# Three second products of a gated feed-forward kernel: from f32 passes to split f16 passes, with low parts added by transfers, and a new program order

## The chip, the cores and the metric

The kernel runs on one core of one Trainium2 chip. A core has TensorE (PE, matrix products; its weight loads are listed as PEld), VectorE (DVE), ScalarE (ACT), GpSimd (POOL) and SyncE (SP, which issues most transfers), each with its own in-order instruction queue; they meet through semaphores. The metric is the device time of one execution in microseconds (us), as a median of several runs. One further execution was taken with the profiler; all rows below come from it.

## What is computed

```python
# q, k, v, f_logit: (4 batches, 8 heads, 768 steps, 48); w_in: (384, 2048); w_out: (2048, 384)
f = 1 / (1 + exp(-f_logit))
for t in range(768):
    state = f[:, :, t, :, None] * state + einsum('bhd,bhe->bhde', k[:, :, t], v[:, :, t])
    y[:, :, t] = einsum('bhd,bhde->bhe', q[:, :, t], state)
x = y.transpose(0, 2, 1, 3).reshape(3072, 384)
h = x @ w_in
out = (h * clip(h + 3, 0, 6) / 6) @ w_out
```

A gated linear attention makes the 3072 rows of `x`; a feed-forward layer with a hard-swish gate follows. Both are wanted in close to f32 precision.

## The kernel before

**Tiling.** The 768 steps are cut into 6 chunks of 128, which with 4 batches gives 24 attention units (0 to 23). Four units, one chunk of all batches, make one group of 512 rows for the feed-forward layer, so there are groups 0 to 5. The 2048 hidden columns are cut into 16 tiles of 128.

**Split precision.** TensorE takes f16 operands in one pass. A f32 operand is therefore held as two f16 parts, `high` (the rounded value) and `low` (the value less its high part), and a product is the sum of three f16 passes: high by high, low weight by high, high weight by low (`P3`). `mm1` (L664) makes a hidden tile so, with 9 matmuls over three blocks of 128 inputs; `relu` (ACT, L674) and `g` (DVE, L678) apply the gate into a f32 tile `t`; `gh` (ACT, L683) makes the high part of `t`, `gl` (DVE or POOL, L693) the low part; `mm2` (L709) multiplies by the 384 outputs, again 9 matmuls of 128x512. Each group's outputs sum up in three PSUM banks `o`, tile after tile.

**The first group.** While attention starts, weights still have to be converted: `ld` loads a weight tile, `z`, `cy`, `mid`, `dif` and `top` turn it into f32 in `wide`, `high` (ACT, L317) and `low` (L320) make its f16 parts; `lowi` and `lowo` make the low part of the first or the second product's columns alone. In group 0, tiles 0 to 4 run in two halves of 256 rows with a second product in f32 (L846), tiles 5 to 7 run whole with a second product in f32 as well: `mm2x` (`mm2_whole`, L720), 3 f32 matmuls of 128x512 straight from `wide` and `t`, each of which stands in the trace as 2 records. Such a tile needs neither `gh` and `gl` nor a low part of its output weights. From tile 8 on, `mm2` takes over. Groups 2 to 5 take another form of the first product (L772, 128x256).

**Attention.** A unit is `tk` (transposes, L516), `kv` (L537), `att` (L497), `qs` (L571) and `av` (L587) on PE, with 16 to 32 small f32 matmuls each, and `mask`, `carry`, `decay` on other engines. `att`, `kv` and `qs`/`av` share two pairs of PSUM banks. While a `qs` has begun to accumulate into a pair, `hold` puts a no-op on PE that waits for PE's own earlier matmul before another step writes that pair.

**The order.** The whole program is one hand-written list of tokens, `ORDER`: it sets the order on every engine, and the number at a token's end says which PSUM bank it takes. `ON_POOL` names the steps that run on POOL. At the end `seed.1` multiplies a block of zeros into a bank (L809), `count` (L985) sums the self-tests of the program, `judge` (L988, L991) decides on a slow fallback, which does not run here. `outs`/`outv`/`outh` copy results out of PSUM, `od`/`odh` send them to memory.

Of the kernel before, what the change touches and what calls it, by code (L numbers as in the profile page):

```python
# [69 lines left out]
mm1.5.4 mask.5 mm2b.4 carry0.6 xh.4 z.7 xl.4 mid.6 dif.6 kmul.7 carry1.6 loadv.5 kv.5.3 ld.8 relu.5 g.5 mm2x.5 cy.7  # L70
top.6 high.6 cy.8 rend.7 tk.7.0 mid.7 dif.7 load.8 lowi.6 carry0.5 top.7 mm1.6.4 ktok.7 qs.5.2 fwd.7 qmul.7 high.7
loadv.7 relu.6 g.6 z.8 decay.7 att.6.0 ld.9 lowi.7 gate.8 av.5 cy.9 z.9 mask.6 mm1.7.4 relu.7 mid.8 dif.8 top.8 mid.9
carry1.5 dif.9 high.8 low.8 mm2x.6 mm1.8.0 g.7 loadq.8 ld.10 top.9 xh.5 cy.10 relu.8 high.9 back.8 rend.8 mm2x.7 ld.11
xl.5 g.8 att.7.2 z.10 cy.11 qs.6.0 kv.7.3 mid.10 load.10 loadv.8 av.6 dif.10 low.9 top.10 z.11 mid.11 gh.8 mm1.9.4
# [5 lines left out]
hole.6 hole.5 mm1.16.4 load.9 mid.15 mm1.17.1 relu.16 carry1.8 relu.17 dif.15 ws1.0 g.16 mm1.20.0 g.17 loadq.11 low.14  # L80
gate.10 xtop.0 gate.9 mm1.18.1 load.11 top.15 relu.18 loadq.10 back.9 high.15 gh.16 av.8 back.10 mm1.14.4 g.18 mm2.13
lowo.4 gh.17 relu.14 low.15 g.14 gh.14 mm1.15.1 mm1.19.4 lowo.6 gh.18 kmul.9 gl.18 rend.9 relu.15 g.15 lowo.3 gh.15
gl.14 gl.15 tk.9.1 lowo.5 lowo.1 mm2.14 fwd.9 mm2.15 gl.16 ktok.9 gl.17 outs.2 loadv.11 lowo.7 outv.1 outs.0 mm1.23.1
mm2.16 gate.11 lowo.2 ws2.0 relu.19 od.0 ws3.0 mm2.17 rend.10 xh.8 g.19 back.11 od.2 kmul.10 relu.20 decay.9 relu.23
kmul.11 hole.8 fwd.10 rend.11 od.1 load.13 qmul.10 xsum.0.2 g.20 g.23 mm1.21.4 relu.21 load.12 xleast.0 tk.10.3 ws4.0
qmul.9 decay.10 ktok.10 mm2.18 gh.19 g.21 mm1.25.3 gh.20 mm1.24.2 gh.21 loadv.10 gate.12 wtop.4 gl.19 relu.24 att.9.1
relu.25 kv.9.0 gl.20 fwd.11 g.25 carry0.9 loadv.12 g.24 wsh.0 load.14 qmul.11 mm1.22.4 gate.13 relu.22 back.12 gh.24
mm2.19 tk.11.3 gl.21 ws1.1 mask.9 gh.23 carry1.9 ktok.11 mm2.20 g.22 qs.9.0 att.11.3 gate.14 loadq.12 gh.25 gl.25 av.9
att.10.2 mm2.21 back.13 gh.22 xh.9 gl.23 kv.11.0 rend.12 kv.10.1 gl.22 mask.10 loadq.13 decay.11 mm1.26.4 ws2.1
mask.11 carry0.10 qs.10.3 ws3.1 carry0.11 carry1.10 kmul.12 kmul.13 fwd.12 qs.11.1 av.10 av.11 relu.26 mm2.22 ws4.1  # L90
xh.10 xh.11 decay.12 rend.13 mm1.27.3 gl.24 carry1.11 relu.27 loadq.14 decay.13 fwd.13 tk.12.2 mm1.28.1 relu.28 hole.9
ktok.12 wsl.0 ws1.2 g.27 tk.13.0 mm2.23 qmul.12 qmul.13 wsh.1 hole.10 att.13.3 ws2.2 g.26 ktok.13 g.28 xtop.1 att.12.1
t0.4 loadv.13 kv.12.2 kv.13.0 back.14 carry0.13 load.15 hole.11 load.16 xsum.1.4 carry0.12 gh.26 mm2.24 gh.27 mm2.25
t0.5 mask.13 carry1.12 t1.4 t1.5 seed.0.2 kmul.14 mm1.30.3 gh.28 t2.4 ws3.2 xleast.1 carry1.13 t2.5 th.4 ws4.2 gate.15
mask.12 gl.26 gl.27 wsl.1 th.5 ws1.3 mm2.26 tl.4 mm1.29.1 tk.14.2 relu.30 mm1.31.0 tl.5 relu.29 rend.14 g.30 p1.8.4
loadv.14 ktok.14 ws2.3 relu.31 p7.8.2 g.29 wsh.2 cs.8 ca.8.2 loadv.17 mm2.27 g.31 p6.8 gh.29 gate.16 fwd.14 qs.13.0
xtop.2 cx.8.3 qs.12.1 p2.8 wsl.2 ws3.3 ra.8 back.15 gl.28 p5.8 av.13 av.12 mm2.28 gh.31 gaw.8 loadq.15 loadq.17 gh.30
ws4.3 rend.15 load.17 ce.8 wsh.3 p4.8 qmul.14 gl.30 gl.29 xh.13 xh.12 p3.8 p8.8 rb.8 rx.8 p7.9.1 decay.14 wsl.3 mm2.29
gl.31 kmul.15 loadq.16 re.8 tk.15.0 gew.8 cs.9 p1.9.4 gbw.8 ca.9.2 mm2.30 fwd.15 loadv.15 gxw.8 back.16 ktok.15
xsum.2.1 mm2.31 p6.9 qmul.15 p7.11.0 xmost.2 gh.33 gh.34 cs.11 xleast.2 p2.9 decay.15 gl.34 hole.13 gh.32 kv.15.1  # L100
kv.14.0 kmul.16 cx.9.3 gl.32 outs.5 load.18 ra.9 hole.12 carry0.14 carry1.14 p4.9 carry0.15 outs.3 carry1.15 p5.9 rx.9
att.14.0 gaw.9 att.15.1 ce.9 outv.4 gate.17 p8.9 mask.14 rend.16 p3.9 mask.15 gh.35 gate.18 qs.15.0 back.17 re.9
qs.14.1 gxw.9 fwd.16 kmul.17 gl.33 gl.35 mm2.32 av.14 av.15 gew.9 p7.10.3 xh.15 rend.17 loadq.18 mm2.33 mm2.34 t0.6
p1.10.4 rb.9 mm2.35 gbw.9 qmul.16 fwd.17 xh.14 loadv.16 back.18 gh.37 gh.38 rend.18 cs.10 decay.16 load.19 kmul.18
ca.10.2 gl.38 hole.15 p6.10 gh.36 tk.17.0 gl.37 p2.10 hole.14 decay.17 tk.16.1 gh.39 cx.10.3 gl.36 p4.10 t1.6 gate.19
fwd.18 ra.10 gaw.10 t2.6 ktok.17 p5.10 ktok.16 att.16.0 kv.16.1 mm2.36 ce.10 t0.7 qmul.17 p8.10 load.20 rx.10 re.10
load.21 qmul.18 back.19 loadv.18 p3.10 mm2.37 rb.10 mask.16 gew.10 carry0.16 carry1.16 p1.11.4 gbw.10 gh.40 att.17.0
gxw.10 kv.17.1 t1.7 th.6 loadq.19 ca.11.2 gl.40 gl.39 mm2.38 gh.42 p6.11 t2.7 carry0.17 xtop.3 carry1.17 gl.42 gate.21
wtop.3 th.7 p2.11 rend.19 tl.6 mm2.39 cx.11.3 gate.20 mm2.40 mask.17 ra.11 gaw.11 tl.7 p4.11 gh.43 rx.11 p5.11 ce.11
tk.18.1 p7.13.0 p8.11 gh.41 gxw.11 gl.43 ktok.18 cs.13 gl.41 xsum.3.3 wtop.8 p3.11 qs.17.1 rb.11 qs.16.0 mm2.41  # L110
loadq.20 re.11 av.17 xmost.3 loadv.19 av.16 xleast.3 p7.12.3 gbw.11 gh.46 gew.11 xh.16 gh.45 p1.12.4 ca.12.2 xh.17
gl.45 mm2.42 loadv.23 att.18.1 kv.18.0 decay.18 gh.44 p2.12 p6.12 back.20 gl.46 cs.12 mm2.43 cx.12.3 carry0.18 gl.44
mask.18 p4.12 ra.12 p5.12 kmul.19 fwd.19 gaw.12 gh.47 mm2.44 decay.19 load.22 ce.12 loadv.22 od.5 back.21 carry1.18
gl.47 rx.12 qmul.19 p3.12 mm2.45 rb.12 p8.12 mm2.46 kmul.20 re.12 gxw.12 qs.18.0 gbw.12 gew.12 hole.16 gh.48 p1.13.4
# [1124 lines left out]
```

## Time and profile before

| | us |
|---|---|
| three runs, median | 456.95 |
| lowest and highest of them | 456.78, 457.9 |
| profiled execution, its own time | 457.2 |
| its span, from the first instruction to the last | 455.5 |
| PE busy | 448.7 (99%) |
| DVE busy | 358.3 (79%) |
| ACT busy | 231.2 (51%) |
| POOL busy | 18.7 (4%) |

Matmuls are pipelined: one lasts longer in the trace than the distance at which the next one starts. How much of PE's time a step takes is therefore read as the distance between its start and the start of the step behind it, not from its duration.

### The profile page before, as it was taken

The numbers are of one execution on the slowest core, as the hardware profiler recorded it, in microseconds if no ns is written. First come the engines' busy times: TensorE is split into PE (matmuls) and PEld (weight loads), VectorE is DVE, ScalarE is ACT, GpSimd is POOL, SyncE is SP. The second block draws the span as 40 slices with busy tenths as digits, with TensorE's granted clock in tenths as the row PEclk, the third lists the DMA queues.
The fourth block names the chain that finished last, engine by engine and source line by source line (L and its number), as shares of the span: only waits on it lengthen the run. The fifth ranks groups of instructions, "written<-read, shape, count | busy, mean of one in ns | idle before, by whom it ended". The sixth has DMA issues, their size and how long they took to land.

```text
span 455.5 us, 12559 instructions
## 1 busy us (share of the span) xinstructions
PE 448.7 (99%) x5449; PEld 291.5 (64%) x5449; DVE 358.3 (79%) x643; ACT 231.2 (51%) x389; POOL 18.7 (4%) x31
## 2 busy tenths in 40 slices
...
PEclk9999999999999999999999999999999999999999
...
GB/s 284 221 257 388 221 192 250 204 167 4 52 130 95 164 47 76 92 3 121 89 1 85 83 150 6 22 142 2 1 10 1 5 30 2 1 115 2 1 0 73
DMA packets 25531, 43.18 MB, mean 95 GB/s; under 512 B 2560, under 2 KB 17408, under 8 KB 25472
## 3 DMA queue, kind: packets, MB, share of 16 engines
...
q14 instruction: 16, 0.13, 0.1%
...
## 4 chain that ended last, share of the span: by engine, by line
PE 96%; DVE 2%; ACT 1%; issue 0%; DVEq 0%; ACTq 0%
PE o L709 35%; PE pair L772 16%; PE single L772 9%; PE pair L664 7%; PE single L664 5%; PE pair L497 3%; PE o L846 3%; PE pair L587 3%; PE pair L571 3%; PE pair L537 2%; PE idle L1071 2%; PE o L720 2%; PE pair L516 2%; PE pair L862 1%; PE o_half L862 1%; PE single L828 1%
## 5 line engine op out<-in xcount | busy, mean ns | idle before, releaser
L709 PE MATMUL o<-gg,weight 128*128 128x512 f16 x744 | 173.4, 379 | 0.0
L709 PEld LDWEIGHTS <-weight 128*128 128x128 f16 x744 | 71.7, 98 | 73.8
L772 PEld LDWEIGHTS <-weight 128*128 128x128 f16 x672 | 65.1, 98 | 13.3 <-issue 0.2
L772 PE MATMUL pair<-xmem,wide 128*128 128x256 f16 x384 | 51.2, 273 | 0.0
L683 ACT ACTIVATE gg<-raws 128x512 f16<-128x512 f32 x64 | 38.4, 624 | 23.9 <-DVE raws L806 8.1
L772 PE MATMUL single<-xmem,weight 128*128 128x256 f16 x384 | 49.8, 273 | 0.2 <-DVE raws L806 0.2
L801 ACT ACTIVATE raws<-pair,half 128x512 f32<-128x512 f32 x32 | 21.5, 684 | 42.3 <-PE pair L772 33.3
L772 PEld LDWEIGHTS <-wide 128*128 128x128 f16 x384 | 36.9, 98 | 8.7 <-DVE single L787 0.6
L801 ACT ACTIVATE raws<-single,half 128x512 f32<-128x512 f32 x32 | 22.0, 687 | 39.8 <-PE single L772 32.2
L664 PEld LDWEIGHTS <-weight 128*128 128x128 f16 x243 | 23.1, 98 | 26.7 <-issue 0.3
L772 PE MATMUL pair<-xmem,weight 128*128 128x256 f16 x288 | 36.5, 273 | 0.0
L806 DVE SCALAR_TENSOR_TENSOR raws<-raws,single 128x512 f32<-128x512 f32 x32 | 21.8, 682 | 18.3 <-ACT raws L801 18.3
L693 DVE TENSOR_TENSOR gg<-raws,gg 128x512 f16<-128x512 f32 x48 | 31.9, 683 | 5.0 <-ACT gg L683 5.0
L664 PE MATMUL pair<-xmem,weight 128*128 128x512 f16 x144 | 33.2, 379 | 0.0
L806 DVE SCALAR_TENSOR_TENSOR raws<-raws,pair 128x512 f32<-128x512 f32 x32 | 21.5, 682 | 12.3 <-ACT raws L801 12.1
L787 DVE TENSOR_TENSOR pair<-pair,raws 128x512 f32<-128x512 f32 x16 | 11.2, 697 | 25.3 <-PE pair L772 17.1
L448 DVE TENSOR_TENSOR_SCAN suffix<-gates,rend 112x516 f32<-112x516 f32 x24 | 29.6, 1235 | 0.1
L428 DVE TENSOR_TENSOR_SCAN suffix<-gates,unit 112x516 f32<-112x516 f32 x23 | 28.0, 1223 | 0.1
L664 PE MATMUL single<-xmem,weight 128*128 128x512 f16 x99 | 23.2, 380 | 0.0
L674 ACT ACTIVATE tg<-pair,half 128x512 f32<-128x512 f32 x16 | 10.9, 686 | 19.5 <-PE pair L664 16.3
L683 ACT ACTIVATE gg<-tg 128x512 f16<-128x512 f32 x24 | 14.4, 626 | 9.0 <-DVE tg L678 5.2
L504 DVE TENSOR_TENSOR a<-pair,causal 128x512 f32<-128x512 f32 x24 | 16.3, 684 | 2.3 <-PE pair L497 1.3
...
## 6 DMA issues: line engine op xcount, KB each, us to landing
...
raws<-w SPq DMA_DIRECT2D x16, 768.0 KB, 5.7
gates<-fg SPq DMA_DIRECT2D x23, 258.5 KB, 3.6
...
wide<-wide SPq DMA_DIRECT2D x32, 24.0 KB, 2.0
...
```

Source lines behind the costliest of these rows:

```text
L428: nc.vector.tensor_tensor_scan(flat(sf)[:, ::-1], gt[:, 1:][:, ::-1], flat(unit)[:, ::-1], 0.0, op0=ALU.mult, op1=ALU.add,)
L448: nc.vector.tensor_tensor_scan(flat(sf), gt[:, :NP * (C + 1)], flat(rend), 0.0, op0=ALU.mult, op1=ALU.add,)
L497: nc.tensor.matmul(d["at"][HC * odd:HC * (odd + 1), e, 2 * n + c], t[rs, 1, n, c, odd], t[rs, 0, n, c, odd], start=not growing[at], stop=T ...
L504: nc.vector.tensor_tensor(d["a"].rearrange("r p e t -> r e p t"), d["at"], causal.unsqueeze(1).unsqueeze(1).broadcast_to([128, 2, NP, HC]) ...
L571: nc.tensor.matmul(d["y"][to:to + 64, odd, n, cs], before[rs, p], t[rs, 0, n, c, odd], start=alone and (odd, e) not in seen, stop=False, s ...
L664: nc.tensor.matmul(h, win[:, f, a, k * 128:(k + 1) * 128], g["xt"][:, k, :g["n"] // C, b], start=i == 0, stop=i == 3 * KT - 1,)
L683: nc.scalar.activation(d["gg"][:, 0], d["t"], AF.Copy)
L693: engine("gl", int(g["name"]) * NF + f).tensor_tensor(d["gg"][:, 1], d["t"], d["gg"][:, 0], op=ALU.subtract)
L709: nc.tensor.matmul(g["o"][m], wout[:, f, a, m * 128:(m + 1) * 128], g[f]["gg"][:, b], start=f == 0 and i == 0, stop=f == NF - 1 and i == 2 ...
L772: nc.tensor.matmul(to[:, n * 256:(n + 1) * 256], weights(q, n, a), g["wide"][:, :, block - 3, b], start=fresh and count == 1, stop=count = ...
L801: nc.scalar.activation(to, src, AF.Relu, bias=half, scale=RISE)
L806: nc.vector.scalar_tensor_tensor(to, to, TOP, src, op0=ALU.min, op1=ALU.mult)
```

## The change

The tiles 5 to 7 of group 0 get the split second product `mm2` in the place of `mm2x`. What this needs is made by new means. `lno` (`conv_minus`) writes the negative of the output weights, rounded to f16, into the place of the low part, on ACT; `lowo` then adds the f32 weights to it by a transfer that POOL issues and that accumulates in its target. In the same way `gn` (`gneg`) writes the negative of `t`, rounded, on ACT, and `gl` adds `t` by such a transfer. There are six of these transfers (`ON_DMA`). `lowo.5` to `lowo.7` stood on DVE before, later in the program.

`apart` and `touch` are new: before a `qs` begins in a pair of banks, PE waits for its own last matmul of an `att`, `kv` or `av` in that pair. PE instructions that wait for PE number 22 before and 40 after.

The first 225 tokens of the order (up to `cy.6`) stay; all behind them stands in a new order. `seed.1` is gone. All else is the same set of steps, with the same banks. Lines behind L193 are up to 33 higher in the changed kernel: `mm2` is L742 there, `gh` L709, `relu` L700.

```diff
+ON_DMA = """
+gl.5 gl.6 gl.7 lowo.5 lowo.6 lowo.7
+""".split()
...
-top.5 cy.6 tk.6.1 ktok.6 mm2a.4 back.7 ld.7 decay.5 high.5 qs.4.2 decay.6 att.5.0 gb.4 av.4 kv.6.1 carry1.4 lowi.5
+top.5 cy.6 qs.4.2 carry1.4 gb.4 mid.6 ld.7 tk.6.1 ktok.6 high.5 cy.7 loadv.5 z.7 back.7 dif.6 decay.6 av.4 kv.5.3 top.6
...
+    def apart(at):
+
+        if touched[at] is not None:
+            after(nc.tensor.nop().ins, touched[at], mybir.DependencyClass.Sync)
+            touched[at] = None
+
+    def touch(at):
+        touched[at] = nc.cur_bb.bb.instructions[-1]
...
+    def conv_minus(f, half):
+        nc.scalar.activation(two(weight[:, f, 1])[:, half], both(f)[:, half], AF.Copy, scale=-1.0)
+
     def conv_low(op, f, half):
+        if f"{op}.{f}" in ON_DMA:
+            nc.gpsimd.dma_start(
+                out=two(weight[:, f, 1])[:, half], in_=both(f)[:, half], accum_op=ALU.add
+            )
+            return
...
         def qs():
             t = chunks[i]
             at, half = pair()
+            apart(at)
...
+    def gneg(g, f):
+        d = g[f]
+        nc.scalar.activation(d["gg"][:, 1], d["t"], AF.Copy, scale=-1.0)
+
     def glow(g, f):
         d = g[f]
+        if f"gl.{int(g['name']) * NF + f}" in ON_DMA:
+            nc.gpsimd.dma_start(out=d["gg"][:, 1], in_=d["t"], accum_op=ALU.add)
+            return
```

PE at the second product of tile 7 in group 0, before. `tg0_7` is the gated f32 tile, `o0_0` to `o0_2` are the group's output banks, L664 is a first product, L497 to L537 are attention.

```order
L664 LDWEIGHTS weight_75
L664 MATMUL pair0_70<-xmem_117,weight_75 128x512
L720 MATMUL o0_0_572<-tg0_7_1042,wide_73 128x512
L720 MATMUL o0_1_573<-tg0_7_1042,wide_73 128x512
L720 MATMUL o0_2_574<-tg0_7_1042,wide_73 128x512
L497 MATMUL pair1_71<-qkf7_792 64x64 x16
L571 MATMUL pair0_70<-qkf6_729,decayed0_104 64x64 x8
L571 MATMUL pair0_70<-qkf6_729,middle0_102 64x64 x8
L537 MATMUL pair1_71<-v7_985,ktok7_964 48x48 x16
```

PE in the changed kernel from the last matmul of tile 5 to the first of tile 8 (`gg0_5`, `gg0_8` are the split tiles; 9 matmuls of tile 8 and then 9 of tile 6, `gg0_6`, follow).

```order
L742 MATMUL o0_2_577<-gg0_5_975,weight_75 128x512
L519 MATMUL pair1_71<-qkf7_795 64x64 x16
L560 MATMUL pair1_71<-v7_931,ktok7_949 48x48 x16
L596 MATMUL pair0_70<-qkf6_732,decayed0_104 64x64 x8
L596 MATMUL pair0_70<-qkf6_732,middle0_102 64x64 x8
L742 LDWEIGHTS weight_75
L742 MATMUL o0_0_575<-gg0_8_1097,weight_75 128x512
```

Three f32 matmuls a tile have become nine f16 ones, and tile 6's stand behind tile 8's; only the last three of a tile's nine read the part that `gl` adds.

ACT in the changed kernel, where tile 6 gets its two parts: `tg0_8` is written by `relu.8`, which waits for the first product of tile 8; then come `gh.6` and `gn.6`, behind which the transfer `gl.6` is released.

```order
L332 ACTIVATE weight_75<-wide_73 128x384
L700 ACTIVATE tg0_7_1072<-single_72,half_95 128x512
L300 ACTIVATE wide_73<-raws_74 128x2x384
L700 ACTIVATE tg0_8_1077<-pair0_70,half_95 128x512
L709 ACTIVATE gg0_6_1089<-tg0_6_979 128x512
L713 ACTIVATE gg0_6_1089<-tg0_6_979 128x512
L709 ACTIVATE gg0_7_1092<-tg0_7_1072 128x512
```

ACT had no step L709 or L713 for tiles 5 to 7 before, and no L332 (`lno`).

POOL before, behind its first two steps (L441 is `kmul`, L457 `decay`, L320 `lowi`, L693 `gl`, L454 `qmul`).

```order
L441 TENSOR_TENSOR qkf6_729<-qkf6_729,suffix0_77 112x512
L320 TENSOR_TENSOR weight_75<-wide_73,weight_75 128x384
L441 TENSOR_TENSOR qkf7_792<-qkf7_792,suffix1_79 112x512
L457 TENSOR_TENSOR decayed1_108<-state3_113,ends_116 112x4x48
L320 TENSOR_TENSOR weight_75<-wide_73,weight_75 128x384
L441 TENSOR_TENSOR qkf8_1065<-qkf8_1065,suffix2_81 112x512
L693 TENSOR_TENSOR gg0_9_1208<-tg0_9_1189,gg0_9_1208 128x512
```

POOL after, the same place.

```order
L463 TENSOR_TENSOR qkf6_732<-qkf6_732,suffix0_77 112x512
L340 TENSOR_TENSOR weight_75<-wide_73,weight_75 128x384
L463 TENSOR_TENSOR qkf7_795<-qkf7_795,suffix1_79 112x512
L336 DMA weight_75<-wide_73 128x384
L718 DMA gg0_5_975<-tg0_5_929 128x512
L340 TENSOR_TENSOR weight_75<-wide_73,weight_75 128x384
L336 DMA weight_75<-wide_73 128x384 x2
L479 TENSOR_TENSOR decayed1_108<-state3_113,ends_116 112x4x48
L718 DMA gg0_6_1089<-tg0_6_979 128x512
L718 DMA gg0_7_1092<-tg0_7_1072 128x512
L726 TENSOR_TENSOR gg0_9_1267<-tg0_9_1262,gg0_9_1267 128x512
L463 TENSOR_TENSOR qkf8_969<-qkf8_969,suffix2_81 112x512
```

Six transfers now stand in POOL's queue among `lowi.7`, `decay.7` and `gl.9`.

## Rows read from the trace of the kernel before

**Rows 1.** The page: busy us (share of the span) and instructions; TensorE clock by slice.
```profile
span 455.5 us, 12559 instructions
...
PE 448.7 (99%) x5449; PEld 291.5 (64%) x5449; DVE 358.3 (79%) x643; ACT 231.2 (51%) x389; POOL 18.7 (4%) x31
...
PEclk9999999999999999999999999999999999999999
```
**Rows 2.** Waits of PE: for whom, us in total, times, longest.
```profile
PE idle L1071 <- DVE blank L247: 1.1, 1, 1.1
PE pair L497 <- DVE qkf L454: 0.5, 1, 0.5
...
PE single L772 <- DVE raws L806: 0.2, 1, 0.2
...
PE pair L587 <- PE pair L571: 0.2, 1, 0.2
```
**Rows 3.** Timeline of PE, tiles 5 to 7: start us, us, engine, line, operation.
```profile
58.65 2.84 PE L720 MATMUL o<-tg,wide 128*128 128x512 f32 x6
61.33 0.55 PE L516 MATMUL pair<-ident,qkf 112*128 112x112 f32 x4
61.71 2.11 PE L664 MATMUL single<-xmem,weight 128*128 128x512 f16 x9
63.75 0.46 PE L571 MATMUL pair<-qkf,decayed 48*64 48x64 f32 x16
...
64.73 0.63 PE L587 MATMUL pair<-a,v 64*48 64x64 f32 x32
65.31 2.10 PE L664 MATMUL single<-xmem,weight 128*128 128x512 f16 x9
67.25 2.74 PE L720 MATMUL o<-tg,wide 128*128 128x512 f32 x6
69.83 2.10 PE L664 MATMUL pair<-xmem,weight 128*128 128x512 f16 x9
71.77 2.74 PE L720 MATMUL o<-tg,wide 128*128 128x512 f32 x6
74.44 0.69 PE L497 MATMUL pair<-qkf 48*64 48x64 f32 x32
```
**Rows 4.** Timeline of PE: a split second product and the step behind it.
```profile
150.22 2.12 PE L709 MATMUL o<-gg,weight 128*128 128x512 f16 x9
152.17 2.11 PE L664 MATMUL pair<-xmem,weight 128*128 128x512 f16 x9
```
**Rows 5.** Timeline of PE early on: a step that waits for the step just ahead.
```profile
24.00 0.46 PE L571 MATMUL pair<-qkf,middle 48*64 48x64 f32 x16
24.64 0.69 PE L587 MATMUL pair<-a,v 64*64 64x64 f32 x32 [0.18 <-PE pair L571]
```
**Rows 6.** Timeline of the end, PE, then DVE.
```profile
451.23 0.38 PE L809 MATMUL pair<-blank 128*128 128x512 f16 x1
451.54 0.23 PE L985 MATMUL pair<-sound,ones 128*1 128x36 f32 x2
...
452.02 0.14 DVE L991 TENSOR_SCALAR flag<-flag 1x1 int32<-1x1 f32 x1
```
**Rows 7.** Busy us of each engine by stretch, clock, DMA share.
```profile
55.00:65.00 10.00, 10.00 (x150) 5.89 (x152) 9.20 (x18) 6.92 (x10) 1.62 (x3) 1.00 0.59 220
65.00:75.00 10.00, 10.00 (x94) 4.74 (x86) 9.54 (x18) 8.18 (x13) 1.90 (x2) 1.00 0.56 208
75.00:85.00 10.00, 10.00 (x150) 5.48 (x140) 9.35 (x16) 7.55 (x12) 1.65 (x2) 1.00 0.64 217
```
**Rows 8.** Groups by line: engine, operation, count, busy us, mean ns.
```profile
L674 ACT ACTIVATE tg<-pair,half 128x512 f32<-128x512 f32 x16 | 10.9, 686 | 19.5 <-PE pair L664 16.3 <-issue 1.6 <-DMA outT<-os 1.6
L683 ACT ACTIVATE gg<-tg 128x512 f16<-128x512 f32 x24 | 14.4, 626 | 9.0 <-DVE tg L678 5.2 <-PE o L709 3.8
...
L320 DVE TENSOR_TENSOR weight<-wide,weight 128x384 f16<-128x384 f32 x13 | 7.1, 552 | 0.3 <-ACT weight L317 0.3
```
**Rows 9.** Transfers by line: count, KB each, median us from issue to landing.
```profile
raws<-w SPq DMA_DIRECT2D x16, 768.0 KB, 5.7
gates<-fg SPq DMA_DIRECT2D x23, 258.5 KB, 3.6
...
wide<-wide SPq DMA_DIRECT2D x32, 24.0 KB, 2.0
```
**Rows 10.** Timeline of POOL: the same operation beside two different stretches of DVE.
```profile
45.11 1.79 POOL L441 TENSOR_TENSOR qkf<-qkf,suffix 112x512 f32<-112x512 f32 x1 [13.98 <-DVE suffix L428]
...
54.74 1.20 POOL L441 TENSOR_TENSOR qkf<-qkf,suffix 112x512 f32<-112x512 f32 x1
```

More of the change, by code (lines that the diff above doesn't have):

```diff
@@ L70 @@
[L70 to L74, printed above, removed]
@@ L80 @@
[L80 to L84, printed above, removed]
@@ L85 @@
[L85 to L114, printed above, removed]
@@ L145 @@
[L145 to L149 removed]
+carry0.2 tk.3.4 ktok.3 mask.2 load.4 gate.4 qs.2.0 hole.1 av.2 xh.2 carry1.2 lowi.0 mm1a.0.4 relua.0 dif.1 qmul.3 top.1
@@ new lines @@
+back.6 top.4 load.7 mm1a.3.4 ld.5 relub.3 mm2a.2 relua.3 ga.3 high.4 gb.3 cy.5 z.5 mask.4 mm2a.3 lowi.4 mm1a.4.1
+relua.4 rend.6 ld.6 mm1b.4.4 relub.4 loadv.6 gate.7 loadq.7 mm2b.3 carry0.4 kmul.6 fwd.6 mid.5 ga.4 dif.5 z.6 qmul.6
+top.5 cy.6 qs.4.2 carry1.4 gb.4 mid.6 ld.7 tk.6.1 ktok.6 high.5 cy.7 loadv.5 z.7 back.7 dif.6 decay.6 av.4 kv.5.3 top.6
+ld.8 z.8 att.5.0 kv.6.1 carry0.6 mask.5 lowi.5 carry1.6 mm1.5.4 relu.5 loadv.7 g.5 mid.7 kmul.7 high.6 lno.5 mm2a.4
+loadv.8 xh.4 decay.5 tk.7.0 ktok.7 lowi.6 dif.7 mm1.6.4 mm2b.4 xl.4 ld.9 carry0.5 ld.10 loadq.8 cy.8 lowo.5 mid.8 gh.5
@@ new lines @@
+gn.5 gl.5 relu.6 top.7 qs.5.2 att.6.0 av.5 high.7 lowi.7 dif.8 hole.4 ld.11 g.6 lno.6 top.8 mask.6 carry1.5 mm1.7.4
+cy.9 rend.7 high.8 low.8 mm1.8.0 fwd.7 xh.5 lno.7 xl.5 relu.7 qmul.7 z.9 lowo.6 relu.8 g.7 mm2.5 gh.6 gn.6 gh.7 g.8
+mid.9 dif.9 gh.8 lowo.7 gl.8 decay.7 cy.10 load.8 z.10 top.9 mid.10 cy.11 z.11 att.7.2 high.9 kv.7.3 carry0.7 qs.6.0
+mm2.8 dif.10 loadq.9 gl.6 mm2.6 mask.7 qs.7.2 top.10 mid.11 gn.7 low.9 load.9 dif.11 av.6 ld.12 ld.14 av.7 xh.6 xl.6
+top.11 gate.9 high.10 low.10 gate.8 gl.7 mm1.9.4 relu.9 high.11 ld.13 g.9 gh.9 mm1.10.1 relu.10 z.12 low.11 cy.12
@@ new lines @@
+low.14 mm1.14.4 relu.18 g.18 fwd.9 relu.14 mm1.15.1 ws1.0 qs.8.2 mm2.13 gate.10 relu.15 gh.17 ws1.1 ws1.2 g.14 qmul.9
+gh.14 ws3.2 gh.18 g.15 gl.18 gl.17 gl.14 tk.9.1 ktok.9 av.8 load.12 gh.15 gate.12 mm2.14 gl.15 back.10 rend.10 mm2.15
+gl.16 decay.10 ws2.0 lowo.2 xh.8 loadv.9 outs.2 ws2.2 mm1.19.4 mm1.23.1 kmul.10 outv.1 outs.0 od.0 back.12 od.2 ws3.1
+mm2.16 relu.19 relu.20 relu.23 od.1 g.19 mm1.21.4 relu.21 carry1.8 g.20 xtop.0 ws4.0 load.11 g.23 xsum.0.2 xleast.0
+tk.10.3 gh.19 lowo.3 decay.9 att.9.1 kv.9.0 mm2.17 fwd.10 qmul.10 xtop.1 gate.11 mask.9 gl.19 ktok.10 back.11 lowo.4
@@ new lines @@
+gh.26 fwd.13 relu.27 loadv.12 mm1.28.1 wsh.0 gate.15 gl.24 qmul.13 relu.28 mm2.22 mm2.23 decay.13 wsl.0 ws3.3 xsum.1.4
+g.27 tk.13.0 ktok.12 ktok.13 ws2.1 decay.12 hole.9 g.28 att.13.3 ws1.3 t0.4 hole.10 kv.12.2 loadv.13 t0.5 t1.5 t2.5
+att.12.1 t1.4 kv.13.0 carry0.12 mm2.24 mm2.25 gate.14 carry1.12 th.5 mask.13 mm1.30.3 mask.12 seed.0.2 gh.27 gh.28
+loadq.14 loadq.15 t2.4 back.14 th.4 carry0.13 carry1.13 mm1.29.1 relu.30 ws2.3 relu.29 kmul.14 ws4.1 back.15 g.30 gl.26
+mm1.31.0 relu.31 load.16 tl.5 mm2.26 tl.4 tk.14.2 g.29 gh.29 g.31 gh.31 kmul.15 qs.13.0 qs.12.1 ktok.14 wsh.1 gl.27
```

124 lines of the change are left out of this document (75 added, 49 removed).

## The prediction

> **What bounds the kernel now.** I read the page first: PE is busy for 448.7 of the span's 455.5 us, at a granted clock of 0.9 or more of full speed, the 2.4 GHz level, in every slice [rows 1]. That alone proves little, since a pipelined matmul counts as busy while the next one already runs, so the waits of PE come second: all that PE waited for, in eight entries, is 2.8 us, of which 1.1 us is the very start and only 0.2 us lies behind the first 26 us (the entry of L772 on DVE) [rows 2]. Third, the timeline of PE shows steps standing back to back [rows 3, 4]. So PE's own work sets the end almost alone. A change here is worth what it takes from PE's list of work, less the waits that it puts into it; what it moves between DVE, ACT, POOL and the transfers counts only where PE comes to wait.
>
> **The change, part by part.**
>
> *The three second products.* A f32 tile is 6 records. With a full-array step ahead and another behind it takes 69.83 - 67.25 = 2.58 us. The other two read 2.68 (an attention step stands ahead) and 2.67 (one stands behind) [rows 3]; entering attention costs the f16 steps as much: 2.04 us from 61.71 to 63.75 against 1.94 from 69.83 to 71.77. So I take 2.58 for all. A split tile takes 152.17 - 150.22 = 1.95 us for nine matmuls [rows 4]. Gain: 3 x (2.58 - 1.95) = 1.9 us, on the path, since PE is the path.
>
> *The zero product at the end* (`seed.1`) starts at 451.23, and `count` behind it at 451.54 [rows 6]: 0.3 us of PE on the way to the end, gone. `count` must then not wait for DVE instead. DVE's last steps (two `wtop`, `xleast.5`, the flags) have moved behind `outv.16`, but PE still has 12 matmuls of 512 and 27 of 256 columns in front of `count` by then; at 0.22 and half of that each, 5.6 us. The DVE work is of the size of 5 us. I take the whole 0.3; if DVE is late, 0.
>
> *The new order.* The list enters small attention matmuls from larger ones 49 times before and 49 times after; an entry costs 0.1 us (above). No change, within 0.2 either way. As PE hardly waits now, a new order has nothing to win and can only add waits.
>
> *The waits of `apart`.* Eighteen more PE instructions wait for PE. The trace prices the worst case: a step right behind the one that it waits for starts 0.64 us after it, where the same step takes 0.28 elsewhere (63.75 to the next 16 records at 64.03, in the same view) [rows 3, 5], so 0.36. Eighteen such waits would be 6.5 us. But in the new order the matmul waited for lies at least four transposes (0.4 us, 61.33 to 61.71 [rows 3]) ahead, mostly 18 or more matmuls. The waits of `hold` at such distances show no entry among PE's waits [rows 2]. I take 0, and 0 to 0.4 for the range.
>
> *ACT and DVE.* ACT gets nine steps, three each of `lno`, `gh` and `gn`; at the 0.63 us of `gh` with 512 columns [rows 8] that is at most 5.7 us. Between 55 and 85 us ACT was busy for 6.9 + 8.2 + 7.6 = 22.7 of 30 us [rows 7]; with all nine there it has 28.4. That is tight but fits, and the conversion of later weights can slide. DVE loses three `lowo`, 3 x 0.55 = 1.7 us [rows 8]. Neither ends PE's waits today; 0.
>
> *The transfers.* No accumulating transfer, and none issued by POOL, is in this trace. What hides them is the distance on PE. The tightest is tile 6: `gl.6` is released behind `relu.8`, `gh.6` and `gn.6`, 0.69 + 0.63 + 0.63 = 1.9 us [rows 8] after the first product of tile 8 ends, and in this time PE does tile 5's second product, 1.95. From then until the first matmul that reads the sum, PE has four attention steps (four such take 65.31 - 63.75 = 1.56 [rows 3]), tile 8's nine matmuls (1.95) and six of tile 6 (1.3): 4.8 us of cover. Tile 5 has about 7, tile 7 more, the three weight transfers 9 and more. The bounds: the smallest transfers inside the core, 24 KB, land 2.0 us after issue; loads of 258.5 KB, the size that `gl` reads, 3.6 us, and 768 KB 5.7 us [rows 9]. The kind is another, so the cost of tile 6 lies between 0 and, with 5.7, 0.9 us; doubling the 3.6 for reading the target too gives 7.2 and a cost of 2.4. I take 3.6 us, the row of its size: hidden, 0. Without that cover each microsecond of it would be one of PE. On its engine, `lowi.7`, `decay.7` and `gl.9` queue behind the transfers on POOL; `decay.7` is wanted by `qs.7`, which stands behind tile 6's product too, so it is covered alike.
>
> The Trainium skill (page DMA: Bandwidth & Descriptors, section Anatomy of one DMA) gives about 2.0 us plus the bytes at 436 KB per us for a transfer that POOL issues, by my estimate 2.6 us for `gl`; by it too the sum would have no wait.
>
> *The end of the program.* Six more transfers mean six more semaphores to wait for at the close. From the last DVE step, which ends at 452.16 [rows 6], to the end of the span at 455.5 there are 3.3 us in which eight transfer queues are closed, a branch taken and five engines met. The rows don't part them: 0 to 0.8 us more, and I take 0.2, as the waits are one of several things there.
>
> *Sum:* -1.9 - 0.3 + 0.2 = -2.0 us. The profiled execution took 457.2 us, which gives 455.2. It lay 0.25 above the median of the runs, 456.95, so I forecast a median of 455.0.
>
> **The rivals.**
>
> *B. The sum for tile 6 comes late.* If the transfer takes 7.2 us, as above, PE waits 2.4 us at its seventh matmul, and the gain is gone: 457.4. For it: in this stretch the transfer engines are busy for 0.56 to 0.64 of the time [rows 7], and an accumulation has to read its target. Against it: 258.5 KB in 3.6 us is a median under load.
>
> *C. ACT becomes the bound.* 28.4 of 30 us leaves no slack for a late operand; if `relu` comes late by 2 us in sum between 55 and 85 us, the time is 457.0. Against it: DVE ran at 9.2 to 9.5 of 10 us there without a PE wait [rows 2, 7].
>
> *D. POOL can't get its transfers out, and the kernel is slower.* POOL gives way where DVE is dense: the same step took 1.79 us at 45.11 and 1.20 at 54.74 [rows 10]. DVE is idle for only 0.5 to 0.8 of each 10 us here [rows 7]. If POOL could prepare a transfer only in DVE's gaps, a microsecond of preparation would last over 10 us; tile 6, with 4.8 us of cover, would wait at least 5.3: 460.3. It decides from 4.8 us between issue and landing on. It speaks against it that POOL's step grew by a half only, though DVE was as dense there. The Trainium skill (page SBUF — State Buffer, section SBUF: two separate sides) states such a rule: while DVE runs an instruction in a mode with two ports, POOL is kept from writing descriptors and the transfer seems blocked; it does not count ordinary two-input f32 steps among those, and no row here shows it.
>
> *E. The waits of `apart` drain PE.* Half of them at 0.36 us is 3.2 us: 458.2. It needs the matmul waited for close ahead, which the order does not have.
>
> **How the numbers follow.** A measurement of this kernel can tell about 0.3% (1.4 us) from no change, so faster means below 455.6 and slower above 458.3. The forecast, 455.0, has 0.62, with a range of its own of 454.2 to 455.6 (no cost at the close and 0.5 of order and spread below, half a microsecond of small waits above). B has 0.14, C 0.08, D 0.11 (its rule by the page as I read it, with few two-port steps, would hide it), E 0.05 (with a little over half of the waits it passes 458.3). Faster is the forecast, 0.62; within 0.3% are B and C, 0.22; slower are D and E, 0.16. The range of 8 in 10 runs from 454.2 to 458.0: it takes in the forecast, B and C, and leaves out D, most of E, and a little below.
>
> **What the profile of the changed kernel would show.** Right: L720 is gone from PE's list and L742 has 27 matmuls more; tiles 5 to 7 take 1.95 us each; PE's waits in 55 to 95 us stay under 0.5 us; `count` starts right behind the last product; `gl.6` lands within 4.8 us of its issue. Wrong: an entry of L742 on a transfer among PE's waits (B, D), of L690 or L742 on ACT (C), of L596 on PE (E), or a `count` that waits for DVE. The forecast falls if PE's waits grow by over 1 us anywhere.

## The result and the profile after

The changed kernel is slower by 1.1%: its median is 462.02 us against 456.98 of the kernel before, a ratio of 1.0112 with a 95% interval of 1.0087 to 1.0138. I had forecast 455.0 and a range of 454.2 to 458.0. The profiled execution took 462.38 us against 457.2.

The page of the changed kernel, as in [rows 1]:

```profile
span 460.6 us, 12618 instructions
...
PE 448.1 (97%) x5457; PEld 290.4 (63%) x5457; DVE 365.1 (79%) x640; ACT 235.4 (51%) x398; POOL 27.1 (6%) x37
```

The granted clock is 1.00 of full speed, the 2.4 GHz level, in every stretch shown below, as before. DVE has three steps less and yet 6.8 us more of busy time. PE, which waited 2.8 us before [rows 2], waits 7.8, in nine entries. Five of them (for whom, us in total, times, longest):

```profile
PE o L742 <- DMA gg<-tg: 2.2, 2, 1.2
PE pair L690 <- DVE weight L340: 1.9, 1, 1.9
...
PE pair L690 <- DVE tg L704: 1.1, 1, 1.1
PE pair L519 <- DVE qkf L476: 0.7, 1, 0.7
...
PE pair L612 <- PE pair L596: 0.2, 1, 0.2
```

Two kinds are new: 2.2 us for the accumulating transfers `gl`, and 3.0 us of first products (L690) that wait for DVE, once for a converted weight and once for a gate. Where they stand, in the timeline of PE (start us, us, engine, line, operation, the wait ahead in brackets), to compare with [rows 3]:

```profile
67.28 1.46 PE L742 MATMUL o<-gg,weight 128*128 128x512 f16 x6
69.79 0.81 PE L742 MATMUL o<-gg,weight 128*128 128x512 f16 x3 [1.05 <-DMA gg<-tg]
...
72.00 3.41 PE L742 MATMUL o<-gg,weight 128*128 128x512 f16 x15
76.59 0.81 PE L742 MATMUL o<-gg,weight 128*128 128x512 f16 x3 [1.18 <-DMA gg<-tg]
...
87.28 5.99 PE L742 MATMUL o<-gg,weight 128*128 128x512 f16 x27
93.11 1.46 PE L690 MATMUL pair<-xmem,weight 128*128 128x512 f16 x6
96.48 0.82 PE L690 MATMUL pair<-xmem,weight 128*128 128x512 f16 x3 [1.92 <-DVE weight L340]
...
109.37 2.12 PE L690 MATMUL pair<-xmem,weight 128*128 128x512 f16 x9 [1.09 <-DVE tg L704]
```

Tile 5 does its first six matmuls at 67.28 and then waits for its low part; tile 6 does the same at the end of the fifteen matmuls from 72.00 on. Behind them PE is back to back until 94.6 us, where six matmuls of the first product of a late tile (the three with its low weights last) are done and the low weights are not.

The stretches (us; PE, PEld, DVE, ACT, POOL busy; clock; share of the transfer engines; GB/s), to compare with [rows 7]:

```profile
55.00:65.00 10.00, 9.83 (x136) 6.01 (x135) 9.97 (x22) 9.49 (x16) 6.64 (x6) 1.00 0.77 213
65.00:75.00 10.00, 8.95 (x131) 4.55 (x130) 9.91 (x17) 9.52 (x15) 2.65 (x4) 1.00 1.08 305
75.00:85.00 10.00, 8.82 (x130) 4.56 (x129) 6.83 (x9) 6.35 (x10) 2.12 (x2) 1.00 0.84 303
```

From 55 to 75 us DVE is idle for less than 0.1 and ACT for 0.5 of each 10 us; the transfer engines, busy for 0.56 to 0.64 of the time before, are at a share of 1.08 between 65 and 75 us.

The second reading is of DVE beside POOL. In the changed kernel, four of POOL's steps between 83 and 94 us, and four of DVE's that meet them:

```profile
83.16 1.27 POOL L726 TENSOR_TENSOR gg<-tg,gg 128x512 f16<-128x512 f32 x1 [7.04 <-ACT gg L709]
85.60 1.19 POOL L463 TENSOR_TENSOR qkf<-qkf,suffix 112x512 f32<-112x512 f32 x1 [1.17 <-DVE suffix L450]
90.39 1.17 POOL L726 TENSOR_TENSOR gg<-tg,gg 128x512 f16<-128x512 f32 x1 [3.61 <-ACT gg L709]
92.73 1.21 POOL L476 TENSOR_TENSOR qkf<-qkf,suffix 112x512 f32<-112x512 f32 x1 [1.17 <-DVE suffix L470]
```

```profile
83.60 1.92 DVE L450 TENSOR_TENSOR_SCAN suffix<-gates,unit 112x516 f32<-112x516 f32 x1
86.02 0.98 DVE L313 TENSOR_SCALAR raws<-top 128x768 int16<-128x768 int16 x1
90.62 2.03 DVE L470 TENSOR_TENSOR_SCAN suffix<-gates,rend 112x516 f32<-112x516 f32 x1
92.93 1.42 DVE L320 TENSOR_TENSOR top<-top,raws 128x768 int16<-128x768 int16 x1
```

Undisturbed, these four forms take 1.22, 0.35, 1.22 and 0.56 us. The first scan starts 0.83 us before POOL's step beside it ends (83.16 + 1.27) and lasts 0.70 too long; the second starts 0.94 before the end of its neighbour and lasts 0.81 too long. DVE's step waits, it seems, until POOL's is over. In the kernel before, POOL's steps mostly met others; here is one of them and a step of DVE beside it:

```profile
81.11 1.18 POOL L693 TENSOR_TENSOR gg<-tg,gg 128x512 f16<-128x512 f32 x1 [7.33 <-ACT gg L683]
```

```profile
81.77 0.37 DVE L552 TENSOR_TENSOR middle<-pair,decayed 112x192 f32<-112x192 f32 x1
```

That one lost nothing. `pair` and `single` lie in PSUM: in these lines a DVE step that takes one operand from there was not slowed by POOL; one that takes both from the SBUF, or the 16-bit step with one operand, was. Between 25 and 120 us I added up what DVE's steps lasted beyond their usual time for their form where a step of POOL's arithmetic lay beside them: less than half a us before; 6.3 us after.

The Trainium skill (page SBUF — State Buffer, section SBUF: two separate sides) says that DVE and GpSimd share one pair of ports, which DVE takes in a mode with two ports, or with two SBUF inputs while a GpSimd step reads the SBUF, and that the later one waits. The trace agrees, with 2.03 us against 1.22 for a scan and 0.37 for the step with a PSUM operand. The prediction named this section for its rule on transfers and passed over this one.

### The profile page after: what moved, and what is told of

Same layout as the page of the kernel before. It is cut to its first block, busy times and chain, and to the rows that moved or that the text cites. A ratio compares the mean times of both kernels' runs of the same rounds, so it can differ in the third digit from the quotient of the medians.

```text
span 460.6 us, 12618 instructions
## 1 busy us (share of the span) xinstructions
PE 448.1 (97%) x5457; PEld 290.4 (63%) x5457; DVE 365.1 (79%) x640; ACT 235.4 (51%) x398; POOL 27.1 (6%) x37
## 4 chain that ended last, share of the span: by engine, by line
PE 85%; DVE 7%; issue 2%; ACT 2%; DMA 2%; POOL 1%; DVEq 0%; POOLq 0%; ACTq 0%
PE o L742 33%; PE pair L805 16%; PE single L805 9%; PE pair L690 4%; PE single L690 3%; PE pair L612 2%; PE pair L519 2%; PE pair L596 2%; PE o L879 2%; PE idle L1104 2%; PE pair L560 2%; DMA gg<-tg 2%; PE pair L539 1%; DVE top L320 1%; PE pair L895 1%
## 5 line engine op out<-in xcount | busy, mean ns | idle before, releaser
L742 PE MATMUL o<-gg,weight 128*128 128x512 f16 x771 | 177.3, 379 | 2.2 <-DMA gg<-tg 2.2
L742 PEld LDWEIGHTS <-weight 128*128 128x128 f16 x771 | 74.5, 98 | 81.6 <-issue 2.8
L805 PEld LDWEIGHTS <-weight 128*128 128x128 f16 x672 | 64.9, 98 | 12.2
L709 ACT ACTIVATE gg<-raws 128x512 f16<-128x512 f32 x64 | 38.4, 625 | 26.5 <-PE o L742 14.9
L690 PEld LDWEIGHTS <-weight 128*128 128x128 f16 x243 | 22.9, 98 | 31.6 <-DVE weight L340 2.4
L690 PE MATMUL pair<-xmem,weight 128*128 128x512 f16 x144 | 33.1, 379 | 3.0 <-DVE weight L340 1.9
L690 PE MATMUL single<-xmem,weight 128*128 128x512 f16 x99 | 23.3, 380 | 0.0
L709 ACT ACTIVATE gg<-tg 128x512 f16<-128x512 f32 x27 | 16.2, 624 | 6.6 <-DVE tg L704 4.8
L546 ACT ACTIVATE ktok<-pair 128x448 f32<-128x448 f32 (+1 forms) x21 | 10.7, 508 | 16.8 <-PE pair L539 16.8
```

Source lines behind the costliest of these rows:

```text
L546: nc.scalar.activation(d["ktok"][:, ns], d["tk"][:, ns], AF.Copy)
L690: nc.tensor.matmul(h, win[:, f, a, k * 128:(k + 1) * 128], g["xt"][:, k, :g["n"] // C, b], start=i == 0, stop=i == 3 * KT - 1,)
L709: nc.scalar.activation(d["gg"][:, 0], d["t"], AF.Copy)
L742: nc.tensor.matmul(g["o"][m], wout[:, f, a, m * 128:(m + 1) * 128], g[f]["gg"][:, b], start=f == 0 and i == 0, stop=f == NF - 1 and i == 2 ...
L805: nc.tensor.matmul(to[:, n * 256:(n + 1) * 256], weights(q, n, a), g["wide"][:, :, block - 3, b], start=fresh and count == 1, stop=count = ...
```

## The experiments

Each kernel was timed against the kernel before on the same chip; its ratio is given with the 95% interval. The first theory, T, was that PE's waits for the transfers also held up DVE, and so caused the waits for DVE further on.

**1. More room for the transfers.** Two tokens move, nothing else (of the tokens between, only those of PE are shown):

```diff
 mm1.8.0
-mm2.5
...
 att.7.2 kv.7.3 qs.6.0
+mm2.5
 mm2.8
-mm2.6
 qs.7.2
...
 mm1.10.1
+mm2.6
```

> Edit: the second product of tile 5 stands behind qs.6 instead of ahead of att.7, and that of tile 6 behind the first product of tile 10, so that every accumulating transfer has over 8 us between issue and first reader; nothing else is changed. Theory T (the transfers are late, and DVE, which is held up while PE waits, brings a second loss): PE's two waits for gg (2.2 us) go, and the two waits of the first product further on (1.9 for a converted weight, 1.1 for the gate of an earlier tile) go with them: 462.0 - 5.0 = 457.0, 0.7 either way. Rival R (the new order alone overloads DVE between 55 and 110 us): the waits for gg go, the 3.0 us behind them stay: 459.8.

459.64 us, 1.0050 (1.0033 to 1.0067). The entry for `gg` is gone from PE's waits; DVE's are not:

```profile
PE pair L519 <- DVE qkf L476: 1.3, 2, 0.9
...
PE pair L690 <- DVE tg L704: 1.1, 1, 1.1
PE pair L690 <- DVE weight L340: 0.6, 1, 0.6
```

The transfers' 2.2 us came back and hardly more (2.8 by the ratios, give or take 1.4). PE reached attention sooner and waited there for DVE instead. Rival R had 459.8; T, with 457.0, falls here. R missed one thing: of the 3.0 us behind the transfers 1.7 stayed, since the wait for the weight went from 1.9 to 0.6.

**2. `gl` of the three tiles on POOL.**

```diff
 ON_POOL = """
-kmul.1 decay.4 kmul.6 lowi.5 kmul.7 decay.7 lowi.7 kmul.8 gl.9 decay.8 gl.11 qmul.8 gl.12 lowo.0 low.14
+kmul.1 decay.4 gl.5 gl.6 gl.7 kmul.6 lowi.5 kmul.7 decay.7 lowi.7 kmul.8 gl.9 decay.8 gl.11 qmul.8 gl.12 lowo.0 low.14
...
 ON_DMA = """
-gl.5 gl.6 gl.7 lowo.5 lowo.6 lowo.7
+lowo.5 lowo.6 lowo.7
```

`gn.5` to `gn.7` are taken out of the order.

> Edit: gl.5 to gl.7 are subtractions on POOL, and the three gn on ACT are left away; lowo.5 to lowo.7 remain accumulating transfers; order as in the changed kernel. Theory T: no second product waits for a transfer; POOL makes a low part in 1.3 to 1.8 us against the 7.0 us of the transfer; ACT is 1.9 us lighter: 457.0, 0.7 either way. Rival R (DVE is overloaded by the order, and POOL's extra 4 us of arithmetic slows it further): the waits for DVE stay at 3 us or grow: 459.8 to 461.

460.52 us, 1.0067 (1.0050 to 1.0083). No wait for a transfer is left, and the two for DVE are to the tenth those of the changed kernel:

```profile
PE pair L690 <- DVE weight L340: 1.9, 1, 1.9
...
PE pair L690 <- DVE tg L704: 1.1, 1, 1.1
```

So they do not come from the waits for the transfers. T is dropped. By itself this run would not settle it, as POOL got more arithmetic in exchange, which R expected to slow DVE; experiment 4 takes the waits away without that.

**3. The transfer by itself, late in the program.**

```diff
+        if op == "echo":
+            nc.gpsimd.dma_start(out=..., in_=gates[0][:, :512], accum_op=ALU.add)
```

> Edit: four more accumulating transfers of 128x512 f32 into f16, between tiles that are no longer used, issued by POOL late in the program, where the transfer engines are almost idle: two one after the other in time, and two back to back. Nothing reads them. H1 (shared engines): one alone lands 2.5 to 4 us after its issue. H3 (own length): 5.5 to 7. If transfers of POOL pass one after the other (H2), the second of the pair lands later than the first by the time that one occupies the engines; else both land together. The time stays at that of the changed kernel, 462.0, as POOL is idle there.

The landing times of the four (first row) against those of `gl` in the changed kernel (second):

```profile
DMA to landing us min/median/max: 3.0/3.3/3.7
```

```profile
DMA to landing us min/median/max: 5.5/7.0/8.4
```

The run took 462.31 us, as expected. In the median the transfer takes 3.3 us there, near the 3.6 that I took. The 7.0 is not its own length. The two issued back to back took no more than 3.7 either, so its place behind another one alone does not give 7 us.

The Trainium skill (page DMA: Bandwidth & Descriptors, section Anatomy of one DMA) would give 2.6 us for it, by the estimate in the prediction; the trace has 3.0 at the least, so the measurement stands. Neither number has the traffic beside it.

**4. Less traffic beside it.** In the changed kernel, the weight loads of six later tiles cut to a quarter:

```diff
-        nc.sync.dma_start(out=raw[:, 1:4 * WN + 1], in_=w[f].bitcast(I16))
+        part = slice(2 * WN - 4, 3 * WN + 4) if 9 <= f <= 14 else slice(0, 4 * WN)
+        nc.sync.dma_start(out=raw[:, 1:4 * WN + 1][:, part], in_=w[f].bitcast(I16)[:, part])
```

> Edit: the changed kernel, but the loads of the weight tiles 9 to 14 bring only a quarter of each tile; the conversion of the rest uses what an earlier tile left in the buffer, so that these weights are not the reference's. Theory H1 (the accumulating transfers, 3.0 to 3.7 us alone, take 7 because they share the transfer engines with these loads): gl lands in 4.5 us or less, PE's waits for gg fall from 2.2 to under 0.5 us; the waits for DVE behind 85 us (3.0) stay at least in part: 459 to 460. Rival H2 (they take 7 us because POOL's transfers pass one after the other): 6 us or more, waits of 1.5 us or more, 461.5.

460.11 us, 1.0059 (1.0041 to 1.0078). The transfers of POOL (count, KB, median us to landing), and the longest wait of PE:

```profile
gg<-tg POOLq DMA_DIRECT2D x3, 128.0 KB, 4.6
weight<-wide POOLq DMA_DIRECT2D x3, 96.0 KB, 6.0
```

```profile
PE pair L691 <- DVE weight L341: 1.9, 1, 1.9
```

With fewer bytes beside them, `gl` lands in 4.6 us and nothing on PE waits for it: H1, though both figures lie just outside what it said (4.5 us or less, 459 to 460). The waits for DVE are the same once more (1.9 and, for the gate, 1.1), without a wait for a transfer and without more work on POOL.

**5. The new order with the old products.**

```diff
-lno.5
...
-lowo.5
...
-gh.5 gn.5 gl.5
...
-mm2.5
+mm2x.5
```

The same for tiles 6 and 7; `lowo.5` to `lowo.7` come later, on DVE.

> Edit: the order of the changed kernel, but the second products of tiles 5 to 7 are the whole f32 ones again, at the places of the split ones; lno, gh, gn and gl of these tiles are left away, and lowo.5 to lowo.7 stand on DVE late, as before. No accumulating transfer is left. Theory D (in the new order DVE's 16-bit steps and scans meet POOL's arithmetic, DVE falls behind, and PE waits for it whatever form the products have): DVE still loses about 5 us beside POOL between 80 and 110 us, PE, with 1.9 us more work, still waits 1 us or more there for a converted weight and for a gate: about 458. Rival P (the loss comes from the split products and from what they need): no such wait over 0.5 us, 456.7 (the time of before less 0.3 for the zero product).

461.11 us, 1.0077 (1.0059 to 1.0094). PE's longest wait, besides which the one for the gate (1.1 us) stands too:

```profile
PE pair L689 <- DVE weight L339: 1.3, 1, 1.3
```

The order alone costs 3.7 us, more than D expected; the split products with all that they need add the last 1.3 (give or take 1.4), where they were to bring 1.9. P falls.

**6. POOL's steps shortened.** On top of experiment 1, five steps of POOL work on an eighth of their columns:

```diff
+            n = 64 if g["name"] == "0" and f in (9, 11, 12) else 512
             engine("gl", int(g["name"]) * NF + f).tensor_tensor(
-                d["gg"][:, 1], d["t"], d["gg"][:, 0], op=ALU.subtract
+                d["gg"][:, 1, :n], d["t"][:, :n], d["gg"][:, 0, :n], op=ALU.subtract
```

(and in the same way `lowo.0` and `low.14`).

> Edit: as the kernel with the two second products moved back, but five of POOL's steps between 80 and 106 us (gl.9, gl.11, gl.12, lowo.0, low.14) work on an eighth of their columns only; what they leave out is filled by the negative high part or by zeros, made by ACT or early by POOL, so that the low parts are not exact. Theory D: DVE gets back the 3.6 us that it lost beside these steps, PE's waits for DVE behind 85 us (1.7 us) go, and the time falls from 459.6 to about 457.7. Rival O (the order asks too much of DVE even without POOL): waits and time stay, 459.6.

458.14 us, 1.0016 (1.0006 to 1.0027), against 1.0050 with the full steps. Two of DVE's steps in experiment 1, and the same two here:

```profile
80.52 1.93 DVE L450 TENSOR_TENSOR_SCAN suffix<-gates,unit 112x516 f32<-112x516 f32 x1
...
102.17 1.89 DVE L320 TENSOR_TENSOR top<-top,raws 128x768 int16<-128x768 int16 x1
```

```profile
82.83 1.22 DVE L451 TENSOR_TENSOR_SCAN suffix<-gates,unit 112x516 f32<-112x516 f32 x1
...
104.17 0.60 DVE L320 TENSOR_TENSOR top<-top,raws 128x768 int16<-128x768 int16 x1
```

Between 25 and 120 us DVE's loss beside POOL falls from 5.8 to 2.1 us, by the same count as above. The wait for `tg` is gone, that for the weight is 0.5, and PE's waits in experiment 1 have no entry on POOL itself. (The profile is of an execution of 460.4 us, 2.3 above the median, with a stop of 1.7 us on PE, at L561, for which it shows no cause; I read only lengths of steps and the waits for DVE from it.) About 1.5 us of the loss (0.0034 of 457, give or take 0.9) was this meeting of POOL and DVE; D holds, a little smaller than it said.

The same trace shows the meeting the other way round. An eighth of `gl` takes POOL 0.31 us at 91.58; where DVE's scan had begun 0.08 us ahead of it, it took four times as long:

```profile
82.91 1.24 POOL L731 TENSOR_TENSOR gg<-tg,gg 128x64 f16<-128x64 f32 x1 [3.40 <-DVE state L584]
```

**7. The meeting, made on purpose in the kernel before.** A fill and six subtractions on POOL behind `lowi.7`:

```diff
+        if op == "crowd":
+            scrap = wide[:, 15]
+            nc.gpsimd.memset(scrap, 0.0)
+            for _ in range(i):
+                nc.gpsimd.tensor_tensor(scrap, scrap, scrap, op=ALU.subtract)
+            continue
```

> Edit: the kernel before, with a fill and six subtractions of 128x384 f32 on POOL behind lowi.7 (at about 65.7 us), in a place of memory that nothing uses then; about 6 us of POOL's time, nothing else is changed. Theory D: DVE's 16-bit steps and its scan last 1.5 to 3 times as long while POOL works (3 us lost between 65.7 and 72.6 us), and as DVE is busy for 9.5 of 10 us there, PE, which hardly waited, now waits 2 us or more for it: 459. Rival: DVE's gaps take it up: 457.0, or DVE isn't slowed at all.

459.19 us, 1.0044 (1.0029 to 1.0059). DVE beside POOL's block from 66.05 to 73.00, where the first three forms take 0.56, 0.35 and 0.96 else, and a step with a PSUM operand:

```profile
66.21 1.07 DVE L308 TENSOR_TENSOR top<-top,raws 128x768 int16<-128x768 int16 x1
...
68.74 0.97 DVE L301 TENSOR_SCALAR raws<-top 128x768 int16<-128x768 int16 x1
...
70.74 1.58 DVE L320 TENSOR_TENSOR weight<-wide,weight 128x768 f16<-128x768 f32 x1
72.24 0.67 DVE L678 SCALAR_TENSOR_TENSOR tg<-tg,single 128x512 f32<-128x512 f32 x1
```

Only `tg`, with an operand in PSUM, keeps its time. PE now waits for the step at 70.74, which makes the low part of tile 8's weights:

```profile
PE pair L664 <- DVE weight L320: 1.1, 1, 1.1
```

It is not that POOL's own next step came late: POOL was idle for 2.07 us before it, until DVE's scan released it. Work that nobody waits for, on an engine that is 4% busy, costs the kernel 1.8 us. D holds.

**8. POOL's steps given to DVE.** On top of experiment 1:

```diff
-kmul.8 gl.9 decay.8 gl.11 qmul.8 gl.12 lowo.0 low.14
+kmul.8 decay.8 qmul.8
```

> Edit: the kernel with the two second products moved back, with gl.9, gl.11, gl.12, lowo.0 and low.14 on DVE instead of POOL; nothing is left out. They are 3.6 us of work on DVE (three at 0.68, one at 0.55, one at 0.95), and DVE lost 3.6 us beside them while POOL did them. Theory D (a step on POOL beside DVE's 16-bit steps and scans costs DVE what it would have cost to do it): the time stays within 0.7 of 459.6. Rival: POOL's steps relieve DVE after all, and the time rises by over 1 us; or DVE is freed, as the collisions also made POOL's results late: below 458.7.

461.52 us, 1.0097 (1.0076 to 1.0118), some 2 us over experiment 1. DVE's scan is back at 1.22, but PE now waits in another place:

```profile
PE o L742 <- DVE gg L726: 3.1, 2, 1.8
```

In DVE's own queue the low parts stand behind steps that the order put ahead of them. On DVE the price was as D had it: it was busy for 364.7 us in experiment 1 and is for 364.3 here, with five steps more. D's time, 459.6 within 0.7, was wrong; the rise of over 1 us is the rival's, though DVE's busy time shows nothing of the relief that it named.

**9. The zero product alone.** `seed.1` is left away in the kernel before, nothing else.

> Edit: the kernel before without the zero product at its end. The sum's term: count starts 0.3 us sooner if DVE's self-tests, whose last step ends at 451.23, are done by then; as they end just when the zero product starts, count may come at 451.3 at the earliest: a gain of 0.2 to 0.3 us, 456.7. Rival: the close waits for something else: 456.95.

456.97 against 457.38 us, 0.9992 (0.9983 to 1.0000): about 0.4, the size of the term, at the edge of what can be told. In the profile `count` starts 0.41 sooner:

```profile
451.13 0.23 PE L985 MATMUL pair<-sound,ones 128*1 128x36 f32 x2
```

**10. The split products in the old order**, with the steps on ACT and the transfers that they need (only PE's tokens are shown).

```diff
-mm2x.5
...
-mm2x.6
 mm1.8.0
+mm2.5
...
-mm2x.7
...
 att.7.2 qs.6.0 kv.7.3
+mm2.6
...
 mm2.8
+mm2.7
```

> Edit: the order of before with the split second products of tiles 5 to 7 alone: lno, gh, gn, gl and lowo of these tiles as in the changed kernel, all six by accumulating transfers, each product moved back until its transfer has 8 us; no waits of apart, and the zero product stays. PE loses 1.9 us of work between 58 and 74 us, DVE 1.7 us of it there. Theory D (DVE's conversion paces this stretch, and the f32 products filled PE while it ran): PE comes to its first products of tiles 6, 8 and 9 before their weights, and waits for DVE or ACT as much as it saved or more: 457 to 459. The prediction's step (PE's work is the path): 457.0 - 1.9 + 0.2 = 455.3.

463.95 us, 1.0142 (1.0097 to 1.0188), with nothing on PE that waits for a transfer:

```profile
PE pair L690 <- ACT weight L330: 2.5, 1, 2.5
PE single L690 <- ACT weight L330: 1.9, 1, 1.9
PE single L690 <- DVE tg L704: 1.7, 1, 1.7
```

This is 5 us above the top of D's range: D had the sign, not the size. All three waits stand between 58 and 71 us, where the f32 products had been: while ACT and DVE converted the next weights, they were the work that PE could do. But two more things changed. The products went further back, by my own placing, and a better one may lose less. And ACT's new steps stand in its queue ahead of the conversions; of the 2.5 us, 1.04 is `gh` and `gn` ahead of the `high` that PE waits for:

```profile
68.74 0.62 ACT L709 ACTIVATE gg<-tg 128x512 f16<-128x512 f32 x1
69.26 0.62 ACT L713 ACTIVATE gg<-tg 128x512 f16<-128x512 f32 x1
69.78 0.83 ACT L330 ACTIVATE weight<-wide 128x768 f16<-128x768 f32 x1
```

What each of the three costs alone is not shown.

## Why the prediction was wrong

**The step that failed first** is in what bounds the kernel: "PE's own work sets the end almost alone". That PE hardly waited was true; that it was alone was not. DVE was busy for 9.2 to 9.5 of each 10 us in the stretch of the change [rows 7]; a chain of conversions ran along with PE, just ahead of it. In the trace of before, the high part of the weights of tiles 5 to 13 was ready 0.7 to 3.0 us before the first product that reads it, and the low part of tile 8, by the line below, at 69.87, where its first reader, the seventh matmul of the product from 69.83 on [rows 3], starts at 71.12:

```profile
68.91 0.96 DVE L320 TENSOR_TENSOR weight<-wide,weight 128x768 f16<-128x768 f32 x1
```

So PE was 1.25 us from waiting there, and 0.7 at tile 11: less than the 1.9 that it was to gain. Less work for PE is only a gain if that chain gets shorter too. Experiment 7 shows it in the kernel before, where POOL's block is the only change: the same step ends at 72.32, 2.45 later, and PE waits 1.06. Experiment 1 shows it in the changed kernel (0.9 us for `qkf` as soon as PE comes sooner). None of my rivals had DVE as what PE waits for, and I put what changes on ACT and DVE at 0, as neither ended PE's waits then.

**The second products** take 1.94 us a tile (27 matmuls from 87.28 to 93.11 are 5.83), as said. The gain of 1.9 was not paid out.

**The new order** I put at 0, by counting PE's entries into attention. That is a view of PE alone. It cost 3.7 us (experiment 5, with the zero product already gone). Part of it is shown: POOL's arithmetic came to lie beside DVE's scans and 16-bit steps, 6.3 us of DVE's time against less than half a us before, and 1.5 us of the kernel's (experiment 6) from the five steps that could be shortened. My reading of [rows 10], that POOL gives way where DVE is dense, does not hold: DVE was about as dense in both places, and what differs is what it did. Beside POOL's 1.79 us at 45.11 stood the line below, with both operands in the SBUF; beside its 1.20 at 54.74 stood DVE's `a<-pair,causal`, with one in PSUM.

```profile
44.89 1.00 DVE L312 SCALAR_TENSOR_TENSOR wide<-top,wide 128x768 int16<-128x768 int16 x1
```

I asked only whether DVE would hold up POOL, not whether POOL would hold up DVE, and I did not ask beside which steps POOL's now stood. The rest of the 3.7 is not settled; what PE waited for there was DVE and steps behind it.

**The transfers** were the term mis-sized: 3.6 us taken, 3.3 alone, 7.0 in place. The bound of 7.2 was right for the wrong reason, as it is the traffic of the loads, not the reading of the target. Tile 5, for which I had about 7 us of cover, waited 1.05 on a transfer of 8.4; this wait lengthened the cover of tile 6 from my 4.8 to 5.9 (69.50 to 75.4), and a transfer of 7.04 made it wait 1.18. Rival B had this mechanism and, for one tile, 2.4 us. It alone would not have passed my range.

**`apart`** was rightly put at 0: the one entry of PE on PE is the 0.2 that stood there before. **Rival D** did not come: POOL's six issues took 0.84 to 1.03 us each, beside a full DVE. **Rival C** did not come in the changed kernel: ACT was at 9.5 of 10 us from 55 to 75, but PE's one entry on ACT is the 0.2 us that stood there before. In experiment 10, with the same steps on ACT, it came in part (2.5 and 1.9 us of waits for ACT).

**The end**: `seed.1` gave 0.4 in experiment 9, where 0.3 was said. The close took 3.8 us (460.6 less 456.8) against 3.3, so 0.5 more instead of 0.2:

```profile
456.64 0.14 DVE L1024 TENSOR_SCALAR flag<-flag 1x1 int32<-1x1 f32 x1
```

The runs part it: the close is 3.6 us in experiment 10 (the transfers, the old order) and 3.6 in experiment 5 (the new order, no transfers). With the six transfers SyncE has 21 semaphore steps there instead of 18, so three more and not six; in the new order the load of the flag at the start of the close takes 0.71 us instead of 0.48. My 0.2 for the semaphores was right in size; the other half I did not foresee.

**The sum again**, in measured terms: -1.9 for the products, -0.4 for the zero product, +0.5 at the close and +5.0 of listed waits (7.8 against 2.8) make +3.2; the span grew by 5.1. Of the 1.9 that are left, some 0.2 is that a wait costs PE more than its entry says: at the five new places the distance between two starts grew by 6.2 us where the waits add to 5.4, and at three old places that are gone (16.12, 18.95 and 264.13 us) it had been 1.2 for 0.6. The other 1.7 is spread over small ones, and I can't name them. In the kernels' times: with the transfers hidden (experiment 1) and five of POOL's steps short (experiment 6) the changed kernel is still 0.7 us above the kernel before, where the sum had it 2.0 below.

Of all kernels tried, only the one without the zero product (experiment 9) stands below the kernel before.
